# Two blocks of cached attention on one core: the last V product as loops, the identity from an iota

## The chip, the cores and the metric

The kernel runs on one core of a Trainium2 chip. The metric is the device time of one execution in microseconds (us), taken as the median of several runs; lower is better. The engines are TensorE (PE in the profile, its weight loads PEld), VectorE (DVE), ScalarE (ACT), GpSimd (POOL) and SyncE (SP), which here issues all DMAs. They run side by side and wait for each other only by semaphores.

## The reference

Two blocks, A and B, are computed one beside the other with their own inputs. Each takes one new token for 2 batch rows, projects it to 32 heads of 192, attends over a cache of 8192 tokens and projects the result back to 640:

```python
q = (x @ wq).reshape(2, 1, 32, 192)              # x: 2 x 1 x 640
scores = einsum("bhqd,bhkd->bhqk", q, k_cache) * 192 ** -0.5
p = softmax(scores)                              # over 8192 tokens
o = einsum("bhqk,bhkd->bhqd", p, v_cache)
out = o.reshape(2, 1, 32 * 192) @ wo             # 640 columns
```

All inputs are bf16; the two outputs stand side by side in 1280 columns. A K or V cache of one block holds 2 x 32 x 8192 x 192 values, about 201 MB; with four caches and the weights the kernel reads 837 MB, each byte once.

## The kernel before, in words

**Units.** The work is cut into 16 units (`NU`), one for each block, batch row and group of 8 heads (`UH`). A unit's K, and its V, is laid over the 128 partitions as 16 partitions for each head with 512 tokens in each. That row is read in three parts (`c` = 0, 1, 2) of 32768 values, 8.4 MB each: 170 whole tokens (`TC`) and 128 values of a token that is cut by the border (the fragments).

**Buffers and loads.** `big` holds three buffers of one part each. The list `loads` gives the order on SP's queue: the K parts of unit 0; then for each unit u a V part of unit u - 1 and a K part of unit u in turn; at the end the three V parts of unit 15. Each load waits until the part that lay in its buffer has been used up. Behind the last V part come the output weights `wo`: block A's in one piece, block B's in five pieces of 29, 11, 5, 2 and 1 rows. Block A's is put into the buffer of V part 0 of the last unit and waits for the signal `("pv", 15, 0)`, which the last matmul of that part gives; block B's goes into the buffer of part 1 and waits for `("pv", 15, 1)`. Last on the queue stand the two stores of the output.

**Start.** GpSimd clears the 33 columns of `tri`, clears `ident`, writes the columns of a triangle with 32 more memsets (L512 to L516), and then clears six other tiles (L518). VectorE makes the four diagonal blocks of the 128 x 128 identity `ident` by subtracting neighbouring columns of the triangle (L521). From the identity come a few small selection tiles (L526 to L548). TensorE turns x with it (L395, `pe_x`), which needs x and the identity. VectorE copies the turned x into `xz` (L292), and the projection follows (`pe_proj`, L402): 16 steps for each block, five matmuls of 384 columns in each. Step 0 is written out, steps 1 to 15 are a loop.

**Scores of a unit.** VectorE multiplies a K part in place by q (L303, L305), TensorE sums groups of 16 by matmuls with the identity (L420, L432), VectorE adds the rest (L313, L317). When all three parts are done, VectorE takes the largest score, GpSimd takes it over the partitions (L346), ScalarE takes the exponentials (L367), and VectorE spreads them into `pb`, with the columns of 8 heads for every token (L340).

**V product of a unit** (`pe_pv`, L450, L456). For each part 85 matmuls: the stationary operand is 40 columns of `pb`, which hold the weights of two tokens for 8 heads each, the moving operand is two tokens of V, 384 columns. All add into the PSUM tile `ops`. Behind the first of the 85 stand one or two small matmuls for the fragments. In the units' loop the V parts of unit u - 1 are worked between the K parts of unit u; for the last unit (`if not real`) the three parts follow each other.

**End.** After part 2 of the last unit its sums are divided by the softmax's denominator and placed into `oall` (L349 to L358, L462), turned (L471), and multiplied by `wo`: block A first (L484, 96 matmuls), then eight idle matmuls (L492), then block B piece by piece (L484, 96 matmuls). ScalarE and VectorE write each block's result to SBUF (L387, L388), and SP stores it.

**How a loop is made.** Every engine has a `_Stream`, a list of operations with their waits, signals and tags. `emit` writes the list out; for each entry `(lo, hi, period)` it is given, `_find` looks for operations whose tags run from `lo` to `hi`, and which agree in name, signals and waits. Two or more such repetitions become one hardware loop (`eng.Fori`), the rest stays unrolled. Inside a loop an operand's place is worked out from the loop's counter:

```python
    def at(self, x, n=1, mult=1):
        return slice(x, x + n) if self.base is None else bass.ds(self.base * mult + x, n)
```

TensorE has three loops before: the projection's steps 1 to 15 for each block, and units 1 to 15.

Of the kernel before, what the change touches and what calls it, by code (L numbers as in the profile page):

```python
# [5 lines left out]
ALU = mybir.AluOpType  # L6
# [113 lines left out]
def build_kernel(nc, blocks, out):  # L120
# [4 lines left out]
    UH = 8  # L125
    HG = Hn // UH
    NQB = NBLK * B
    NU = NQB * HG
    LASTU = NU - 1
    TP = Sk * UH // 128  # L130
    NCH = 3
    ROW = TP * Dh // NCH
    TC = ROW // Dh
    FR = ROW - TC * Dh
    OFF = (0, Dh - FR, FR)
# [8 lines left out]
    QW = 2 * Dh  # L144
    WR = Hn * Dh // 128
    GP = Dh // WR
    HP = 32
    MP = HP + UH
    HM = Hn // 2
    XM = HM - 1  # L150
    PQ0 = -100
    XW = XM + 128
    PO = 128 - UH
    scale = float(Dh) ** -0.5
# [3 lines left out]
    with ExitStack() as es:  # L158
# [10 lines left out]
        pb = sb("pb", [128, TP * UH], BF16)  # L169
        sc = sb("sc", [128, TP], F32)  # L170
# [3 lines left out]
        ident = sb("ident", [128, 128], BF16)  # L174
# [12 lines left out]
        rc = sb("rc", [UH, 1], F32)  # L187
# [3 lines left out]
        xz = pb[:, 0:XZE].rearrange("p (k c m) -> p k c m", k=NBLK, c=DC)  # L191
        x4 = pb[0:NQB, 1536:1536 + D]
        zero = pb[:, 2304:2304 + Dh]
        tri = pb[0:HP, 2560:2560 + HP + 1]
        out_sb = pb[0:HP + B, 0:D]
        o_all = qc[:, 0:Dh]

        ops = ps("ops", [128, 512], F32)
# [8 lines left out]
        bufs = [big[:, i * ROW:(i + 1) * ROW] for i in range(NBUF)]  # L207
# [7 lines left out]
        S_pe = _Stream("pe", sem("s_pe"), reg, 1)  # L215
        S_act = _Stream("act", sem("s_act"), reg, 1)
        S_dve = _Stream("dve", sem("s_dve"), reg, 1)
        S_pool = _Stream("pool", sem("s_pool"), reg, 1)
# [17 lines left out]
        buf = {}  # L236
# [9 lines left out]
        for blk, rows in ((0, (WR,)), (1, (29, 11, 5, 2, 1))):  # L246
            r = 0
# [32 lines left out]
        def fragments(b, c):  # L280
            if c == 0:
                return [(0, 0, FR, bufs[b][:, ROW - FR:ROW])]
            if c == 1:
                return [(0, FR, Dh, bufs[b][:, 0:Dh - FR]), (1, 0, Dh - FR, bufs[b][:, ROW - (Dh - FR):ROW])]
            return [(1, Dh - FR, Dh, bufs[b][:, 0:FR])]
# [154 lines left out]
        def col(s):  # L440
            return 64 * (s // 8) + 32 * (s % 2) + 8 * (s % 8 // 2)

        def pe_pv(u, c):
# [14 lines left out]
                return ins  # L458
            return fn

        def pe_pl(u):
            return lambda eng: eng.matmul(oacc_all[:, 0:Dh], place[:, S_pe.at(UH * u, 128, UH)], o_sb[:],  # L462
                                          start=False, stop=True, skip_group_check=True)
# [45 lines left out]
        for blk in range(NBLK):  # L509
            S_sp.add(out_dma(blk), waits=[("oev", blk, 1), ("oev", blk, 0)])  # L510

        S_pool.add(lambda eng: eng.memset(tri, 0.0), sig=("tri0",))  # L512
        S_pool.add(lambda eng: eng.memset(ident[:], 0.0))
        for n in range(1, HP + 1):
            S_pool.add((lambda n: (lambda eng: eng.memset(tri[0:n, n:n + 1], 1.0)))(n),
                       waits=[("tri0",)] if n == 1 else [], sig=("tri",) if n == HP else None)  # L516
        for n, t in enumerate((pb[:, 0:XZE], zero, esel[:], onehot[:], turn[:], place[:])):
            S_pool.add((lambda t: (lambda eng: eng.memset(t, 0.0)))(t), sig=("init", n))  # L518

        for n in range(128 // HP):  # L520
            S_dve.add((lambda r: (lambda eng: eng.tensor_tensor(ident[r, r], tri[:, 1:HP + 1], tri[:, 0:HP], ALU.subtract)))  # L521
                      (slice(HP * n, HP * n + HP)), waits=[("tri",)], sig=("id1",) if n == 128 // HP - 1 else None)
        for blk in range(NBLK):
            for b in range(B):
                S_dve.add(dve_xz(blk, b), waits=[("px",), ("init", 0)], sig=("xz",) if (blk, b) == (1, 1) else None)
        S_dve.add(lambda eng: eng.tensor_reduce(em[:], ident[:].rearrange("p (m t) -> p t m", t=GP), AXL.X, ALU.add),  # L526
                  waits=[("id1",)], sig=("em",))
# [38 lines left out]

        streams = {"pe": S_pe, "dve": S_dve, "act": S_act, "pool": S_pool}
        slots = {e: {} for e in streams}

        def put(eng, slot, name, fn, waits, lag=0):  # L570
            slots[eng].setdefault(slot, []).append((name, fn, [w for w in waits if w is not None], lag))

        for u in range(NU + 1):
            real, old = u < NU, u >= 1
            v = u - 1

            def red(c, k):
                put("dve", u, ("r", c, k), dve_red(u, c, k), [("s", u, c, k), ("sp", u - 1) if u else None])

            def turn_out():  # L580
                put("dve", u, ("rc", -1), dve_rc, [("pv", v, NCH - 1), ("of", v - 1)])
                put("dve", u, ("oh", -1), dve_ohi, [("of", v - 1)])
                put("dve", u, ("os", -1), dve_osum, [("oh", v)])
                put("act", u, ("of", -1), act_of, [("os", v), ("rc", v), ("pl", v - 1)])

            def v_part(c):
                if c == 0:
                    put("pe", u, ("l", -1), pe_l, [("exp", v), ("sp0", v), ("os", v - 1), ("rc", v - 1)])
                put("pe", u, ("pv", c, -1), pe_pv(v, c), [("v", v, c), ("sp", v) if c else None])

            if not real:
                for c in range(NCH):
                    v_part(c)
                turn_out()
                put("pe", u, ("pl", -1), pe_pl(v), [("of", v)])
                continue
            put("dve", u, ("su", 1), dve_su(u + 1), [("q", u)])
            for c in range(NCH):
                if old:
                    v_part(c)  # L600
                for k in range(NSUB):
                    if old and c == NCH - 1 and k == 3:
                        turn_out()
                    w = [("k", u, c), ("qe", u), ("sl", u - 1, NCH - 1) if u and c == 0 else None]
                    put("dve", u, ("m", c, k), dve_mul(u, c, k), w)
                    put("pe", u, ("s", c, k), pe_sum(u, c, k), [("m", u, c, k), prev(u, c, k)])
                    if old and c == NCH - 1 and k == 3:
                        put("pe", u, ("pl", -1), pe_pl(v), [("of", v)])
                    n = NSUB * c + k - 3
                    if n >= 0:  # L610
                        red(n // NSUB, n % NSUB)
                put("pe", u, ("sl", c), pe_rest(u, c),
                    [("m", u, c, NSUB - 1), ("rl", u - 1) if u and c == 0 else None])
            c = NCH - 1
            for k in range(NSUB - 3, NSUB):
                red(c, k)
            put("dve", u, ("rl",), dve_rest, [("sl", u, c)])
            put("dve", u, ("mx",), dve_max, [("rl", u)])
            put("dve", u, ("mp",), dve_mp, [("mx", u), ("ar", u - 1) if u else None, ("negm",)])
            put("dve", u, ("nm",), dve_nm, [("ar", u)])  # L620
            put("dve", u, ("nb",), dve_nb, [("nm", u), ("exp", u - 1) if u else None])
            put("pe", u, ("q", 1), pe_q, [("su", u + 1), ("qe", u)])
            put("pool", u, ("ar",), pool_ar, [("mp", u), ("nm", u - 1) if u else None])
            put("act", u, ("qe", 1), act_q, [("q", u + 1), ("m", u, NCH - 1, NSUB - 1)])
            put("act", u, ("exp",), act_exp, [("nb", u), ("l", v) if u else None])
            g0, g1 = -(-TC // 8), TP // 8
            put("dve", u, ("sp0",), dve_spread([(0, g0), (g1 - 1, g1)]),
                [("exp", u), ("pv", v, NCH - 1) if u else None, ("mask",)])
            put("dve", u, ("sp",), dve_spread([(g0, g1 - 1)]), [])

        def full(name, u):
            lag = name[-1] if name[0] in ("su", "q", "qe", "l", "pv", "rc", "oh", "os", "of", "pl") else 0
            rest_ = name[1:-1] if lag else name[1:]
            return (name[0], u + lag) + rest_

        for e, S in streams.items():
            order = [n for n, *_ in slots[e][1]]
            have = {n for n, *_ in slots[e][0]}
            after = {}
            at = None  # L640
            for n in order:
                if n in have:
                    at = n
                else:
                    after.setdefault(at, []).append(full(n, 0))
            for u in sorted(slots[e]):
                for n, fn, waits, _ in slots[e][u]:
                    S.add(fn, waits=waits, sig=full(n, u), tag=(u, n),
                          pre=after.get(None, ()) if u == 0 and n == slots[e][0][0][0] else (),
                          post=after.get(n, ()) if u == 0 else ())  # L650

# [13 lines left out]
        with nc.Block() as block:  # L665
            @block.sync
            def _(eng):
                S_sp.emit(eng)

            @block.gpsimd  # L670
            def _(eng):
                S_pool.emit(eng)

            @block.vector
            def _(eng):
                S_dve.emit(eng, [(1, NU, 1)])

            @block.scalar
            def _(eng):
                S_act.emit(eng, [(1, NU, 1)])  # L680

            @block.tensor
            def _(eng):
                S_pe.emit(eng, [(PQ0 + 1, PQ0 + HM, 1), (PQ0 + 2 * HM + 1, PQ0 + 3 * HM, 1), (1, NU, 1)])

        for blk in range(NBLK):
            nc.scalar.wait_ge(*reg["odone", blk])
# [49 lines left out]
```

## Time and profile before

| | us |
|---|---|
| median of 3 runs (lowest, highest) | 1937.39 (1936.87, 1938.21) |
| the profiled execution, whole | 1937.25 |
| its span, first to last instruction | 1935.4 |
| TensorE busy | 1532.6 |
| weight loads busy, beside the matmuls | 784.1 |
| VectorE busy | 1119.2 |
| ScalarE busy | 29.6 |
| GpSimd busy | 9.4 |

The profile is of one execution, the whole time of which is 1.85 us above its span. The time beside a group of instructions is their busy time; matmuls are pipelined, and the ends that the trace gives them are modelled, so the distance between starts says more about their pace than the length of one. "Issue" as a cause of idle time means that the engine waited for nothing that the profile shows. The granted clock is the share of full speed that TensorE's clock gate allowed, 0.929 on average over the span.

### The profile page before, as it was taken

How to read it: one execution, taken by the hardware profiler on the slowest of the kernel's cores; microseconds unless marked ns; L12 is line 12 of the kernel's file. 1: busy time of each engine (PE TensorE's matmuls, PEld its weight loads, DVE VectorE, ACT ScalarE, POOL GpSimd, SP SyncE). 2: the span in 40 equal slices, each digit the busy share in tenths (PEclk: the TensorE clock that was granted, in tenths of full speed). 3: DMA queues.
4: the chain of work that ended last, by engine and by line, in shares of the span. 5: the costliest groups of instructions: out<-in, count | busy, mean ns of one | idle time of the engine just before them, and what ended most of it. 6: DMA issues, size and time to landing. Idle time of an engine off the chain costs nothing.

```text
span 1935.4 us, 18767 instructions
## 1 busy us (share of the span) xinstructions
PE 1532.6 (79%) x8255; PEld 784.1 (41%) x8256; DVE 1119.2 (58%) x841; ACT 29.6 (2%) x75; POOL 9.4 (0%) x60
## 2 busy tenths in 40 slices
PE   4778787887888778797787878878797777878778
PEld 2334343443434434353343434433343343434435
DVE  0785555846566485546846566485546846565450
ACT  0000000000000000000000000000000000000000
POOL 0000000000000000000000000000000000000000
PEclk9999898898999999999999999999998988999889
DMA  9999999999999999999999999999999999999998
GB/s 412 435 441 434 434 436 433 433 435 433 433 435 433 433 433 433 433 433 435 437 435 435 433 433 433 433 433 433 433 434 437 435 437 433 433 433 436 433 432 380
DMA packets 15147, 836.94 MB, mean 432 GB/s; under 512 B 1688, under 2 KB 1824, under 8 KB 2208
## 3 DMA queue, kind: packets, MB, share of 16 engines
q1 hardware_dynamic: 15136, 836.78, 99.8%
q8 instruction: 9, 0.15, 0.0%
q14 instruction: 2, 0.02, 0.0%
HBM read 836.77 MB, written 0.01 MB: 432 GB/s over the span
## 4 chain that ended last, share of the span: by engine, by line
PE 35%; DMA 34%; DVE 17%; issue 13%; DVEq 0%; POOL 0%; ACT 0%; SPq 0%; ACTq 0%; POOLq 0%
PE ops L450 22%; DMA big<-in_B_k_cache_dram 17%; DMA big<-in_A_k_cache_dram 14%; DVE big L305 12%; PE scps L420 10%; DVE sc L313 3%; DMA big<-in_B_wo_dram 2%; PE scps L402 2%; PE rest L432 1%; DMA pb<-in_B_x_dram 1%; DVE pb L340 1%; DVE rmax L321 0%; POOL mg L346 0%; PE ops L456 0%; DVE o_hi L352 0%
## 5 line engine op out<-in xcount | busy, mean ns | idle before, releaser
L420 PE MATMUL scps<-big,ident 128*128 128x512 bf16 x2880 | 716.5, 408 | 284.0 <-DVE sc L313 268.1
L305 DVE TENSOR_TENSOR big<-big,qt 128x6144 bf16<-128x6144 bf16 (+1 forms) x240 | 847.5, 3548 | 0.0
L450 PE MATMUL ops<-big,pb 128*40 128x384 bf16 x4080 | 710.7, 336 | 0.0
L420 PEld LDWEIGHTS scps<-big,ident 128*128 128x128 bf16 x2880 | 285.1, 103 | 700.6 <-DVE sc L313 332.9
L450 PEld LDWEIGHTS ops<-big,pb 128*40 128x40 bf16 x4080 | 414.5, 103 | 272.3 <-issue 28.9
L303 DVE TENSOR_TENSOR pad<-big,qt 128x128 bf16<-128x128 bf16 (+1 forms) x64 | 11.9, 207 | 633.7 <-DMA big<-in_B_k_cache_dram 341.5
L313 DVE TENSOR_REDUCE sc<-scps 128x32 f32<-128x512 f32 x240 | 161.0, 681 | 31.2 <-PE scps L420 31.2
L340 DVE TENSOR_TENSOR pb<-sc,mask 128x704 bf16<-128x704 f32 (+2 forms) x96 | 76.3, 863 | 14.1 <-ACT sc L367 14.1
L438 PE MATMUL ops<-rs,mask 128*8 128x1 f32 x32 | 3.1, 167 | 84.8 <-DVE pb L340 84.8
L432 PEld LDWEIGHTS rest<-big,ident 128*128 128x128 bf16 x576 | 44.4, 101 | 13.9 <-issue 4.5
L432 PE MATMUL rest<-big,ident 128*128 128x160 bf16 x576 | 49.1, 236 | 0.0
L438 PEld LDWEIGHTS ops<-rs,mask 128*8 128x8 f32 x32 | 1.6, 90 | 88.4 <-DVE pb L340 82.8
L402 PE MATMUL scps<-big,pb 128*128 (+1 forms) x160 | 31.7, 338 | 6.8 <-issue 6.8
L358 ACT ACTIVATE o_sb<-o_hi,rc 8x192 bf16<-8x192 f32 x16 | 7.3, 454 | 1537.2 <-DVE o_hi L355 1537.2
L349 DVE RECIPROCAL rc<-ops 8x1 f32<-8x1 f32 x16 | 2.3, 147 | 41.4 <-PE ops L450 41.4
L295 DVE TENSOR_TENSOR su<-esel,onehot 128x144 bf16<-128x144 bf16 x17 | 5.1, 300 | 35.8 <-PE outps L410 35.8
L402 PEld LDWEIGHTS scps<-big,pb 128*128 (+1 forms) x160 | 15.7, 99 | 22.6 <-issue 15.1
L395 PE MATMUL rest<-ident,pb 4*128 4x4 bf16 x5 | 0.4, 178 | 21.9 <-DMA pb<-in_B_x_dram 21.9
L346 POOL PARTITION_ALL_REDUCE mg<-mp x16 | 5.8, 365 | 1855.2 <-DVE mp L324 1855.2
L317 DVE TENSOR_REDUCE sc<-rest 128x30 f32<-128x480 f32 x16 | 10.5, 657 | 7.3 <-PE rest L432 7.3
L367 ACT ACTIVATE sc<-sc,nb 128x512 f32<-128x512 f32 x16 | 11.5, 721 | 32.8 <-DVE nb L330 32.8
L292 DVE CAST pb<-rest 128x5 bf16<-128x5 f32 x4 | 0.4, 171 | 19.5 <-PE rest L395 19.5
(66 smaller groups left out, 131.5 us busy)
## 6 DMA issues: line engine op xcount, KB each, us to landing
big<-in_B_wq_dram SPq DMA_DIRECT2D x1, 7680.0 KB, 37.4
big<-in_A_wo_dram SPq DMA_DIRECT2D x1, 7680.0 KB, 29.2
big<-in_A_wq_dram SPq DMA_DIRECT2D x1, 7168.0 KB, 20.3
big<-in_B_wo_dram SPq DMA_DIRECT2D x1, 4640.0 KB, 27.7
big<-in_B_wo_dram SPq DMA_DIRECT2D x1, 1760.0 KB, 31.4
big<-in_B_wo_dram SPq DMA_DIRECT2D x1, 800.0 KB, 32.8
big<-in_A_wq_dram SPq DMA_DIRECT2D x1, 512.0 KB, 3.8
big<-in_A_k_cache_dram SPq DMA_DIRECT2D x24, 38.4
```

What stands on the lines that cost most here:

```text
L303: eng.tensor_tensor(pad[:, t, lo:hi], src, qt[:, 0, lo:hi], ALU.mult)
L305: return eng.tensor_tensor(t, t, qt[:].broadcast_to([128, size(k), Dh]), ALU.mult)
L313: return lambda eng: eng.tensor_reduce(sc[:, lo:lo + SUB], scps[bank(u, c, k)][:], AXL.X, ALU.add)
L317: eng.tensor_reduce(dst, rest[:, 0:NCH * REST, :].rearrange("p (c t) g -> p c t g", c=NCH), AXL.X, ALU.add)
L340: ins = eng.tensor_tensor(dst[:, lo:hi, a], src[:, lo:hi, a].unsqueeze(3).broadcast_to(shape), mask[:].unsqueeze(1).unsqueeze(1).broadcast ...
L346: return eng.partition_all_reduce(mg[:], mp[:], 128, bass.bass_isa.ReduceOp.max)
L358: return eng.activation(o_sb[:], o_hi[:], ACTF.Identity, scale=rc[:])
L367: return eng.activation(sc[:], sc[:], ACTF.Exp, bias=nb[:], scale=scale, accum_out=rs[:])
L402: ins = eng.matmul(flat[0][:, 0:QW], xz[:, blk, c, S_pe.at(m, 128)], wq_t[blk][:, c, S_pe.at(QW * m, QW, QW)], start=(blk == 0 and m == 0 ...
L420: ins = eng.matmul(scps[bank(u, c, k)][:], ident[:], t[:, :, j * DG:(j + 1) * DG], start=(j == 0), stop=(j == NJ - 1))
L432: ins = eng.matmul(rest[:, lo:lo + n, :], ident[:], src[:, :, j * DG:(j + 1) * DG], start=(j == 0), stop=(j == NJ - 1))
L450: ins = eng.matmul(ops[0:MP, 0:QW], pb[:, j0:j0 + MP], bufs[b][:, OFF[c] + j * QW:OFF[c] + (j + 1) * QW], start=(c == 0 and j == 0), stop= ...
```

## The change

Two edits that do not touch each other.

In the last unit, part 0 and part 1 of the V product are each split into a head (`pe_pv_head`: the first of the 85 matmuls and the fragments) and 21 passes (`pe_pv_pass`) of four matmuls. The passes carry tags of their own, from 1000 for part 0 and 1100 for part 1, and `emit` gets a range for each, so that they can become loops of 21 turns. The operands of a pass move on by 64 columns of `pb` and by 1536 columns of the V buffer at each turn. The last pass gives the signal `("pv", 15, c)`; the other passes give signals too, for which nobody waits. Part 2 stays as it was, and so do the units in the units' loop.

The identity: GpSimd writes `p - column` as f32 into the first 128 columns of `sc` with one iota, and VectorE compares it with zero into `ident` with one instruction. The tile `tri`, its 33 memsets, the memset of `ident` and the four subtractions go.

```diff
+    PV0 = 1000
+    VP = 4
+    VN = (TC // 2 - 1) // VP
...
-        tri = pb[0:HP, 2560:2560 + HP + 1]
+        diff = sc[:, 0:128]
...
+        def pe_pv_head(u, c):
+            b = buf["v", u, c]
+
+            def fn(eng):
+                j0 = col(TC * c)
+                ins = eng.matmul(ops[0:MP, 0:QW], pb[:, j0:j0 + MP], bufs[b][:, OFF[c]:OFF[c] + QW],
+                                 start=(c == 0), stop=False, skip_group_check=True)
+                for t, lo, hi, src in fragments(b, c):
+                    j0 = col(NCH * TC + t)
+                    ins = eng.matmul(ops[0:UH, lo:hi], pb[:, j0:j0 + UH], src, start=False, stop=False,
+                                     skip_group_check=True)
+                return ins
+            return fn
+
+        def pe_pv_pass(u, c, i):
+            b = buf["v", u, c]
+
+            def fn(eng):
+                for n in range(VP):
+                    j = 1 + VP * i + n
+                    ins = eng.matmul(ops[0:MP, 0:QW], pb[:, S_pe.at(col(TC * c + 2 * j), MP, 16 * VP)],
+                                     bufs[b][:, S_pe.at(OFF[c] + j * QW, QW, VP * QW)],
+                                     start=False, stop=True, skip_group_check=True)
+                return ins
+            return fn
...
-        S_pool.add(lambda eng: eng.memset(tri, 0.0), sig=("tri0",))
-        S_pool.add(lambda eng: eng.memset(ident[:], 0.0))
-        for n in range(1, HP + 1):
-            S_pool.add((lambda n: (lambda eng: eng.memset(tri[0:n, n:n + 1], 1.0)))(n),
-                       waits=[("tri0",)] if n == 1 else [], sig=("tri",) if n == HP else None)
+        S_pool.add(lambda eng: eng.iota(diff, [[-1, 128]], base=0, channel_multiplier=1,
+                                        allow_small_or_imprecise_dtypes=True), sig=("diff",))
...
-        for n in range(128 // HP):
-            S_dve.add((lambda r: (lambda eng: eng.tensor_tensor(ident[r, r], tri[:, 1:HP + 1], tri[:, 0:HP], ALU.subtract)))
-                      (slice(HP * n, HP * n + HP)), waits=[("tri",)], sig=("id1",) if n == 128 // HP - 1 else None)
+        S_dve.add(lambda eng: eng.tensor_scalar(ident[:], diff, 0.0, None, ALU.is_equal), waits=[("diff",)], sig=("id1",))
...
             if not real:
+                put("pe", u, ("l", -1), pe_l, [("exp", v), ("sp0", v), ("os", v - 1), ("rc", v - 1)])
                 for c in range(NCH):
-                    v_part(c)
+                    if c == NCH - 1:
+                        put("pe", u, ("pv", c, -1), pe_pv(v, c), [("v", v, c)])
+                        continue
+                    put("pe", u, ("pvh", c), pe_pv_head(v, c), [("v", v, c), ("sp", v) if c else None])
+                    for i in range(VN):
+                        n = ("pv", c, -1) if i == VN - 1 else ("pvt", c, i)
+                        put("pe", u, n, pe_pv_pass(v, c, i), [])
+                        tags["pe", u, n] = (PV0 + 100 * c + i, ("pvt", c))
...
-                S_pe.emit(eng, [(PQ0 + 1, PQ0 + HM, 1), (PQ0 + 2 * HM + 1, PQ0 + 3 * HM, 1), (1, NU, 1)])
+                S_pe.emit(eng, [(PQ0 + 1, PQ0 + HM, 1), (PQ0 + 2 * HM + 1, PQ0 + 3 * HM, 1), (1, NU, 1)]
+                          + [(PV0 + 100 * c, PV0 + 100 * c + VN, 1) for c in range(NCH - 1)])
```

More of the change, by code (lines that the diff above doesn't have):

```diff
@@ L151, in build_kernel @@
     PQ0 = -100
+    PV0 = 1000
+    VP = 4
+    VN = (TC // 2 - 1) // VP
+    assert VP % 4 == 0 and 1 + VN * VP == TC // 2
     XW = XM + 128
@@ L568, in build_kernel @@
         slots = {e: {} for e in streams}
+        tags = {}
         def put(eng, slot, name, fn, waits, lag=0):
@@ L647, in build_kernel @@
                 for n, fn, waits, _ in slots[e][u]:
-                    S.add(fn, waits=waits, sig=full(n, u), tag=(u, n),
+                    S.add(fn, waits=waits, sig=full(n, u), tag=tags.get((e, u, n), (u, n)),
                           pre=after.get(None, ()) if u == 0 and n == slots[e][0][0][0] else (),
```

## The prediction

> **What bounds the kernel now.** I read the page first (span, transfers, queues), then the chain of waits, then the timeline at both ends, where the change lies, and last the windows view for the clock. The page says that the transfers set the time:
>
> ```profile
> span 1935.4 us, 18767 instructions
> ...
> GB/s 412 435 441 434 434 436 433 433 435 433 433 435 433 433 433 433 433 433 435 437 435 435 433 433 433 433 433 433 433 434 437 435 437 433 433 433 436 433 432 380
> DMA packets 15147, 836.94 MB, mean 432 GB/s; under 512 B 1688, under 2 KB 1824, under 8 KB 2208
> ## 3 DMA queue, kind: packets, MB, share of 16 engines
> q1 hardware_dynamic: 15136, 836.78, 99.8%
> q8 instruction: 9, 0.15, 0.0%
> ```
>
> 836.9 MB at 432 GB/s is 1937 us, the whole span; of 40 slices only the first and the last move less. So an edit in mid-kernel is worth nothing unless it holds a transfer back, and an edit behind the last loads is worth what TensorE needs there. The V product of the last unit lies there. First its part 0 (timeline: start, length, engine, line, operation, count, in brackets the idle time before and what ended it), then what TensorE does to the end:
>
> ```profile
> 1869.19 15.40 PE L450 MATMUL ops<-big,pb 128*40 128x384 bf16 x85
> 1869.49 0.16 PEld L450 LDWEIGHTS ops<-big,pb 128*40 128x40 bf16 x1 [0.16 <-issue]
> ```
>
> ```profile
> 1884.67 13.99 PE L450 MATMUL ops<-big,pb 128*40 128x384 bf16 x85
> 1898.59 0.22 PE L456 MATMUL ops<-big,pb 128*8 128x128 bf16 x1
> 1898.74 13.83 PE L450 MATMUL ops<-big,pb 128*40 128x384 bf16 x84
> ...
> 1915.58 8.36 PE L484 MATMUL outps<-big,oT 128*2 128x320 bf16 x96
> 1924.10 1.67 PE L492 MATMUL ops<-big,ident 128*128 128x512 bf16 x7 [0.16 <-issue]
> 1926.27 5.69 PE L484 MATMUL scps<-big,oT 128*2 128x320 bf16 x80 [0.50 <-DMA big<-in_B_wo_dram]
> 1932.19 1.45 PE L484 MATMUL scps<-big,oT 128*2 128x320 bf16 x16 [0.23 <-DMA big<-in_B_wo_dram]
> ```
>
> From 1869 to 1933.6 TensorE hardly stops: parts 0, 1 and 2 of V, the last unit's sums, block A's output product, the idle matmuls, block B's output product. That the transfers still lead is seen only in the bracket before block B's product, and it holds 0.50 us. This small lead is all that hides anything added to TensorE here. Two transfers hang on parts 0 and 1, wo of block A and wo of block B. Their issues, and the times to landing:
>
> ```profile
> 1884.45 0.33 SPq L256 DMA_DIRECT2D big<-in_A_wo_dram  x1
> 1898.53 2.24 SPq L256 DMA_DIRECT2D big<-in_B_wo_dram  x5
> ```
>
> ```profile
> big<-in_A_wo_dram SPq DMA_DIRECT2D x1, 7680.0 KB, 29.2
> ...
> big<-in_A_wq_dram SPq DMA_DIRECT2D x1, 512.0 KB, 3.8
> ```
>
> Block A's wo lands at 1884.45 + 29.2 = 1913.7. Its 7680 KB (7.86 MB) take 18.2 us at 432 GB/s, so until about 1895.5 the queue still had V to move: its issue has 11 us of lead. Block B's is issued 15 us ahead of 1913.7. The 512 KB load, into an empty queue, takes 3.8 us where 432 GB/s would take 1.2; so 2.6 us is the start of a transfer.
>
> **The loops.** The change turns the 84 matmuls behind the head of part 0, and of part 1, into 21 passes of four, with addresses from the loop's counter. No matmul goes. What a pass costs beyond its matmuls is seen in the projection, such a loop on the same engine, with five matmuls of the same 384 columns in a pass (timeline, then the windows view, whose third column from the end is the granted clock):
>
> ```profile
> 22.78 6.49 PE L402 MATMUL scps<-big,pb 128*128 128x384 bf16 x30 [0.53 <-issue]
> ...
> 40.88 3.50 PE L402 MATMUL scps<-big,pb 128*128 x20 [0.26 <-issue]
> 44.64 0.98 PE L402 MATMUL scps<-big,pb 128*128 x5 [0.26 <-issue]
> ```
>
> ```profile
> 44.64:59.78 15.14, 11.84 (x60) 5.78 (x61) 0.00 (x0) 0.00 (x0) 0.00 (x0) 1.00 0.96 416
> 1868.50:1872.10 3.60, 3.60 (x14) 1.66 (x14) 2.66 (x2) 0.00 (x0) 0.00 (x0) 0.50 1.05 455
> 1849.00:1862.00 13.00, 8.72 (x43) 3.87 (x44) 11.27 (x11) 0.45 (x1) 0.00 (x0) 1.00 1.00 434
> ```
>
> Twelve passes (60 matmuls) fill 15.14 us, 1.26 us each. In part 2 above, 84 matmuls take 13.83 us with one every 0.1625 us and 0.33 us for the last, so five need 0.81 us: 0.45 us of each pass is waiting, and "issue" says that no data was missing. Inside a pass nothing waits: 0.98 is four starts of 0.1625 and the last one's 0.33. So matmuls with computed addresses are handed over every 0.16 us or faster, and the rest belongs to turning back. If handing over one takes s and the turn e, a pass of five is 5s + e = 1.26, and one of four 1.26 − s. At most s is 0.16, by what was just read. At least it is about 0.065, the pace of matmuls with fixed addresses in block B's product:
>
> ```profile
> 1926.27 3.76 PEld L484 LDWEIGHTS scps<-big,oT 128*2 128x2 bf16 x58 [0.99 <-DMA big<-in_B_wo_dram]
> ```
>
> I take s = 0.12, about the middle: **1.14 us for a pass of four**. The ends are 1.10 (s = 0.16) and 1.26 (s = 0). If all of the pass went with the number of its matmuls it would be 1.01; the gaps, which stand at the turn alone, speak against that.
>
> The Trainium skill, page "Advanced Engine Details and Errata", section "Control Flow Timing", gives about 108 ns for a compare-and-branch. By that figure alone the 40 turns below would be 4.3 us and the whole change some +3 us; the projection's 0.45 us per pass disagrees.
>
> Four matmuls need 0.65 us, so each turn leaves 0.49 us idle. 21 passes have 20 turns (entering and leaving show no gap: the 20 matmuls from 40.88 are one loop's last pass, five unrolled ones and the next loop's first two passes). Two loops: 40 × 0.49 = 19.6 us. From this goes what the slow clock hides. Part 0 starts at 0.50 of the clock with matmuls 0.32 us apart, nine of them (15.40 − 0.33 = 9 × 0.32 + 75 × 0.1625). Four at that pace last longer than a pass, so two to three turns are covered, 1.1 us. TensorE is then 18.5 us later, 8.7 from part 0 and 9.8 from part 1. Does the clock stay up when the array works 0.65 of 1.14 us, 57%? In the scores of the last unit, busy 8.72 of 13 us, it was 1.00, and in the projection, at 64%, too. I take full clock.
>
> Now who waits. Part 0's end releases wo of A on SP's queue: 1893.2 in place of 1884.45; with its start of 2.6 us it arrives just as the queue runs dry at 1895.5. Part 1's end releases the five pieces of wo of B: 1917.0 in place of 1898.5, behind A's landing at 1913.7, so the DMA engines stop there for some 6 us. On SP only the output's stores are queued behind. B's rows have landed by 1917.0 + 2.6 + 18.2 = 1937.8. TensorE asks for them later than that: part 2 ends 18.5 us late, block A's product begins at 1934.1 and the idle matmuls end at 1944.3. Block B then waits for no row: 95 × 0.065 + 0.3 = 6.5 us, where it took 7.37 (1926.27 to 1933.64). With the lead of 0.50 that gives back 1.3 us. The end moves by 18.5 − 1.3 = **17.2 us**, by TensorE's chain; the late transfer hides under it.
>
> **The identity.** It is off the path. Groups of the first 66 us, and two rows of the timeline:
>
> ```profile
> L518 POOL MEMSET pb<- 128x1430 bf16 (+1 forms) x2 | 1.5, 763 | 0.0
> L550 ACT ACT_TABLE_LOAD x1 | 1.3, 1283 | 0.7 <-PEq L722 0.7
> L515 POOL MEMSET pb<- 1x1 bf16 (+31 forms) x32 | 1.1, 91 | 0.0
> L521 DVE TENSOR_TENSOR ident<-pb 32x32 bf16<-32x32 bf16 x4 | 0.7, 166 | 2.1 <-POOL pb L515 2.1
> ```
>
> ```profile
> 3.75 0.30 POOL L518 MEMSET place<- 8x248 bf16 x1
> 21.90 0.27 PEld L395 LDWEIGHTS rest<-ident,pb 4*128 4x128 bf16 x5 [21.90 <-DMA pb<-in_B_x_dram]
> ```
>
> Its first reader waits for x until 21.90; the identity is ready at 2.1 + 0.7 = 2.8 us. 34 memsets and four subtractions go, an iota and a comparison come. The trace has no iota: by the nearest rows of GpSimd it lies between 0.09 us (a small memset) and 1.5 us (the two large ones); I take 0.5. The six memsets behind it on the same queue, done at 4.05 now, and the comparison end within 6 us. No gain and no loss reaches the end, unless the iota took some 19 us; then the cover is gone and each further us delays the projection.
>
> **Sum.** The profiled execution took 1937.25 us (the span and 1.85 around it), 0.14 below the runs' median of 1937.39. 1937.25 + 17.2 = **1954.4 us**.
>
> **Rivals.** *Turns hidden, so not slower* (0.07): the sequencer is ahead of the array and turning back costs nothing. For it: the projection's first 30 matmuls, the unrolled five and five passes, run without one gap, as the first nine of them are at half pace. Against it: every later pass has its gap. It decides at 0.65 us per pass; below, the time stays at 1937.3, and the only gain is in instructions not fetched (0.15 MB of 837 for all of them). The Trainium skill's 108 ns would end beside this case.
>
> *Half clock* (0.05): the gaps let the throttle fall. A pass then takes 4 × 0.32 = 1.28 us and a part 26.9, in place of 15.1 and 13.7; part 2 loses 1.4 in warming: 26.4 − 1.3 = +25.1, 1962.4 us. The projection's clock speaks against it.
>
> *Code fetched again* (0.03): each turn drops what was fetched ahead and waits for a transfer, at most the 3.8 us of the 512 KB load. In one of the two loops: 20 × (3.8 − 0.49) = 66 us more, about 2020. Against it: the two projection loops and the unit loop turn back 42 times, and q8 has nine packets in all. The Trainium skill, page "Runtime: NRT & Kernel Launch", section "Instruction fetch mechanics", states such a stall for targets outside the fetched window; the nine packets agree that short loops stay inside.
>
> *Slow iota* (0.01), over 19 us: above 1954. *No loop made* (0.01): if the stream's search did not find the passes alike, the code would stay unrolled, 1937.3; tag, signal and waits are the same in all 21.
>
> **How the numbers follow.** Forecast 0.83. Passes of 1.01 give 40 × 0.36 − 0.8 − 1.3 = +12.3, 1949.5 us; 1.10 gives 1952.9; 1.26 gives 40 × 0.61 − 1.4 − 1.3 = +21.7, 1959.0; half clock 1962.4. So the range is 1949 to 1962.5 and leaves out 0.12. About 0.2%, 3.9 us, is what a measurement of this kernel can tell from no change: same are the hidden turns and no loop, 0.08; slower 0.91; faster 0.01.
>
> **What would show it.** Right: groups of four matmuls 1.14 us apart in parts 0 and 1 with "issue" in the brackets; wo of A issued at 1893, wo of B at 1917, a dip in DMA from 1914; no wait for DMA before block B's product; nine packets or fewer in q8. Wrong: passes of 0.65 us; a clock near 0.5 in the loops; a first matmul that waits for the identity and not for x.

## The result and the profile after

The changed kernel takes 1952.89 us (median of 6 runs, 1951.47 to 1954.52), the kernel before 1937.16 us in the same comparison (6 runs, 1936.75 to 1938.21): ratio 1.008, 95% interval 1.0067 to 1.0093, 15.7 us slower. The prediction had 1954.4 in a range of 1949 to 1962.5. The profiled execution took 1953.05 us, its span is 1951.6.

On the page after, the transfers are the same bytes, but the last slice (48.8 us) has fallen from 380 to 243 GB/s: nothing moves from 1912 to 1916, and after 1937 next to nothing is left to move.

```profile
GB/s 423 430 430 436 431 438 431 431 441 430 438 431 433 439 430 439 430 434 438 430 439 430 435 437 433 437 430 437 435 434 434 431 437 435 434 435 430 442 426 243
DMA packets 15146, 836.93 MB, mean 429 GB/s; under 512 B 1688, under 2 KB 1824, under 8 KB 2208
## 3 DMA queue, kind: packets, MB, share of 16 engines
q1 hardware_dynamic: 15136, 836.78, 99.1%
q8 instruction: 8, 0.13, 0.0%
```

The timeline of parts 0 and 1 shows the passes (L485 is the pass's matmul, L470 the head of part 1, L454 that of part 2; the first row is eight passes in which the view shows no gap), and the windows view the clock in the same stretches (third column from the end; the last is GB/s):

```profile
1869.99 8.18 PE L485 MATMUL ops<-big,pb 128*40 x32
...
1878.44 0.82 PE L485 MATMUL ops<-big,pb 128*40 x4 [0.27 <-issue]
...
1891.71 0.82 PE L485 MATMUL ops<-big,pb 128*40 x4 [0.27 <-issue]
1892.55 0.32 PE L470 MATMUL ops<-big,pb 128*40 128x384 bf16 x1
...
1892.95 0.83 PE L485 MATMUL ops<-big,pb 128*40 x4
1894.02 0.82 PE L485 MATMUL ops<-big,pb 128*40 x4 [0.24 <-issue]
...
1915.03 0.82 PE L485 MATMUL ops<-big,pb 128*40 x4 [0.26 <-issue]
1915.76 0.33 PE L454 MATMUL ops<-big,pb 128*40 128x384 bf16 x1
```

```profile
1869.98:1875.09 5.11, 5.11 (x18) 2.51 (x18) 1.98 (x2) 0.00 (x0) 0.00 (x0) 0.50 0.95 410
1880.63:1891.70 11.07, 8.35 (x40) 3.82 (x40) 0.00 (x0) 0.00 (x0) 0.00 (x0) 1.00 0.97 420
1895.10:1915.00 19.90, 14.83 (x72) 6.89 (x72) 0.00 (x0) 0.00 (x0) 0.00 (x0) 1.00 0.81 349
1912.00:1916.00 4.00, 3.15 (x17) 1.44 (x15) 0.00 (x0) 0.00 (x0) 0.00 (x0) 1.00 0.00 0
1914.30:1918.50 4.20, 3.94 (x24) 2.15 (x24) 0.00 (x0) 0.00 (x0) 0.00 (x0) 1.00 0.49 141
```

From 1878.44 to 1891.71 lie 12 passes, 1.106 us each; from 1894.02 to 1915.03 lie 19, also 1.106. The clock is at 1.00 once the first 5 us are over, and at 0.50 in these. The last two rows are the hole in the transfers: nothing for 4 us, and 141 GB/s in the 4.2 us around the issue of block B's weights. Then the issues of the output weights, and TensorE's end:

```profile
1892.56 0.33 SPq L260 DMA_DIRECT2D big<-in_A_wo_dram  x1
1915.89 2.59 SPq L260 DMA_DIRECT2D big<-in_B_wo_dram  x5
```

```profile
1933.01 8.36 PE L514 MATMUL outps<-big,oT 128*2 128x320 bf16 x96
1941.53 1.67 PE L522 MATMUL ops<-big,ident 128*128 128x512 bf16 x7 [0.16 <-issue]
1943.13 6.68 PE L514 MATMUL scps<-big,oT 128*2 128x320 bf16 x96
```

Block B's product (L514) now runs in one piece of 96, and the bracket with the DMA wait is gone: TensorE's chain sets the end (the row of 1933.01 is block A's product). From row to row, before and after:

| step | before | after | later by | added here |
|---|---|---|---|---|
| first matmul behind part 0's head | 1869.19 | 1869.99 | 0.80 | 0.80 |
| part 0 done, wo of A issued | 1884.45 | 1892.56 | 8.11 | 7.31 |
| part 1 done, wo of B issued | 1898.53 | 1915.89 | 17.36 | 9.25 |
| idle matmuls begin (second of them) | 1924.10 | 1941.53 | 17.43 | 0.07 |
| block B's product begins | 1926.27 | 1943.13 | 16.86 | -0.57 |
| its last matmul ends | 1933.64 | 1949.81 | 16.17 | -0.69 |
| span | 1935.4 | 1951.6 | 16.2 | 0.03 |

The time outside the span was 1.45 us where it had been 1.85, so the profiled executions differ by 15.8 us.

At the start, the iota came much later than the memsets had, and x was still the last input:

```profile
9.52 0.24 POOL L542 IOTA sc<- 128x128 f32 x1 [9.09 <-issue]
9.71 1.48 POOL L545 MEMSET pb<- 128x1430 bf16 x2
9.79 1.84 DVE L547 TENSOR_SCALAR ident<-sc 128x128 bf16<-128x128 f32 x1 [9.79 <-POOL sc L542]
...
22.91 0.27 PEld L399 LDWEIGHTS rest<-ident,pb 4*128 4x128 bf16 x5 [22.91 <-DMA pb<-in_B_x_dram]
```

### The profile page after: what moved, and what is told of

It reads as the page before. It is cut to its first block, busy times and chain, and to the rows that moved or that the text cites. A ratio compares the mean times of both kernels' runs of the same rounds, so it can differ in the third digit from the quotient of the medians.

```text
span 1951.6 us, 19029 instructions
## 1 busy us (share of the span) xinstructions
PE 1547.7 (79%) x8255; PEld 787.9 (40%) x8256; DVE 1120.7 (57%) x838; ACT 29.6 (2%) x75; POOL 8.4 (0%) x27
## 4 chain that ended last, share of the span: by engine, by line
PE 41%; DMA 29%; DVE 16%; issue 13%; DVEq 0%; POOL 0%; ACT 0%; ACTq 0%; SPq 0%; POOLq 0%
PE ops L454 22%; DMA big<-in_B_k_cache_dram 14%; DMA big<-in_A_k_cache_dram 14%; PE scps L424 12%; DVE big L309 10%; DVE sc L317 3%; PE ops L485 2%; PE scps L406 2%; PE rest L436 2%; DMA pb<-in_B_x_dram 1%; DVE pb L344 1%; DVE rmax L325 1%; PE outps L514 0%; PE scps L514 0%; POOL mg L350 0%
## 5 line engine op out<-in xcount | busy, mean ns | idle before, releaser
L454 PE MATMUL ops<-big,pb 128*40 128x384 bf16 x3910 | 682.0, 336 | 0.0
L454 PEld LDWEIGHTS ops<-big,pb 128*40 128x40 bf16 x3910 | 397.3, 103 | 261.6 <-issue 28.2
L307 DVE TENSOR_TENSOR pad<-big,qt 128x128 bf16<-128x128 bf16 (+1 forms) x64 | 11.9, 206 | 616.5 <-DMA big<-in_B_k_cache_dram 333.1
L485 PE MATMUL ops<-big,pb 128*40 x168 | 36.3, 348 | 9.2 <-issue 9.2
L485 PEld LDWEIGHTS ops<-big,pb 128*40 x168 | 17.1, 102 | 28.0 <-issue 20.9
```

The source lines that it names most:

```text
L307: eng.tensor_tensor(pad[:, t, lo:hi], src, qt[:, 0, lo:hi], ALU.mult)
L454: ins = eng.matmul(ops[0:MP, 0:QW], pb[:, j0:j0 + MP], bufs[b][:, OFF[c] + j * QW:OFF[c] + (j + 1) * QW], start=(c == 0 and j == 0), stop= ...
L485: ins = eng.matmul(ops[0:MP, 0:QW], pb[:, S_pe.at(col(TC * c + 2 * j), MP, 16 * VP)], bufs[b][:, S_pe.at(OFF[c] + j * QW, QW, VP * QW)], s ...
```

## The experiments

All times are medians, beside runs of the kernel before on the same chip (1937.08 to 1937.27 us). Every diff is against the changed kernel. The theory under test: the loss is what TensorE's sequencer cannot get ahead with in the 40 turns; the rivals are the new identity, a price by matmul, a turn that always stops the array, and the late transfer.

**The two halves apart.** First the loops with the old identity:

```diff
-        S_pool.add(lambda eng: eng.iota(diff, [[-1, 128]], base=0, channel_multiplier=1,
-                                        allow_small_or_imprecise_dtypes=True), sig=("diff",))
+        S_pool.add(lambda eng: eng.memset(tri, 0.0), sig=("tri0",))
+        S_pool.add(lambda eng: eng.memset(ident[:], 0.0))
...
-        S_dve.add(lambda eng: eng.tensor_scalar(ident[:], diff, 0.0, None, ALU.is_equal), waits=[("diff",)], sig=("id1",))
...
```

> The two loops alone, the identity made as before. Theory: the whole loss sits in the turns of the two loops (40 turns with about 0.45 us idle each, less what the half clock at the start of part 0 and the lead before block B's product hide), so +15 to +16 us against before, the same as the full change. Rival: the new start (x landed at 22.9 and not at 21.9 us in the changed kernel, and the last unit's V product began 0.8 us later) is part of it, then about +14.5 us and x back at 21.9.

Measured: 1952.82 us, ratio 1.0079 (1.0065 to 1.0093), the whole loss. Then the identity alone:

```diff
                 for c in range(NCH):
-                    if c == NCH - 1:
-                        put("pe", u, ("pv", c, -1), pe_pv(v, c), [("v", v, c)])
-                        continue
...
+                    v_part(c)
```

> The identity alone, the V product unrolled as before. Theory: nothing to see, within 0.5 us of before, although the iota begins only at about 9.5 us; the first matmul still waits for x. Rival: +0.8 to +1.0 us, with x landing a microsecond later, if the late start of GpSimd's first iota takes something from the transfers.

Measured: 1937.33 us, ratio 0.9999 (0.9990 to 1.0008), although its iota began at 9.80 us and x was used at 22.90, as in the full change. The identity adds nothing; the rival that gave it a microsecond is out.

**Longer passes.** Same matmuls, fewer turns.

```diff
-    VP = 4
+    VP = 12
```

> Passes of 12 matmuls, 7 passes, 6 turns in each loop. From passes of five (1.262 us, projection) and four (1.105 us, the changed kernel) the theory has 0.157 us for each matmul and 0.48 us for a turn: a pass of 12 takes 2.36 us, 0.41 idle at each turn, 2.5 us for part 1, about 0.7 for part 0, less 1.25 of lead: +2 us against before. Rival: the cost goes with the number of matmuls that have computed addresses, whatever the number of turns; then a pass takes 3.3 us and the end moves by +14 us as with passes of four.

Measured: 1939.44 us, ratio 1.0012 (1.0003 to 1.0021), +2.2 us. The timeline: part 0 in one row, in part 1 a first row of three passes without a gap, then single ones from 1893.39 to 1900.43, three periods of 2.347 us.

```profile
1870.15 16.57 PE L485 MATMUL ops<-big,pb 128*40 x84
...
1886.96 6.19 PE L485 MATMUL ops<-big,pb 128*40 x36
1893.39 2.12 PE L485 MATMUL ops<-big,pb 128*40 x12 [0.24 <-issue]
...
1900.43 2.12 PE L485 MATMUL ops<-big,pb 128*40 x12 [0.24 <-issue]
```

The slope between passes of 4 and 12 is (2.347 - 1.106) / 8 = 0.155 us for a matmul, and 0.48 is left for the turn: the theory's numbers, and no price by matmul alone. That the first passes of part 1 show no gap says that the sequencer was still ahead from part 0, where in this trace 17 matmuls were 0.32 us apart.

```diff
-    VP = 4
+    VP = 28
```

> Passes of 28 matmuls, 3 passes, 2 turns in each loop. Theory: a pass of 28 x 0.157 + 0.48 = 4.87 us against 4.55 without loop, 0.3 idle at a turn, part 0 wholly covered by the half clock, part 1 +0.65 us, which is less than the 1.25 us of lead: no change against before, within 0.5 us. Rival (cost by matmul): +14 us again.

Measured: 1936.81 us, ratio 1.0000 (0.9991 to 1.0009). Part 1 is one row, as long as unrolled (13.83 us for part 2 before): no turn shows.

```profile
1884.69 13.83 PE L485 MATMUL ops<-big,pb 128*40 x84
```

**What a turn consists of.** Passes of four whose operands do not move; all but four of the 84 column pairs are left out.

```diff
-                    ins = eng.matmul(ops[0:MP, 0:QW], pb[:, S_pe.at(col(TC * c + 2 * j), MP, 16 * VP)],
-                                     bufs[b][:, S_pe.at(OFF[c] + j * QW, QW, VP * QW)],
+                    ins = eng.matmul(ops[0:MP, 0:QW], pb[:, col(TC * c + 2 * j):col(TC * c + 2 * j) + MP],
+                                     bufs[b][:, OFF[c] + j * QW:OFF[c] + (j + 1) * QW],
```

> Both loops with passes of four as in the change, but every pass uses the operands of the first one (it leaves out all but four of the 84 column pairs), so that no address is worked out in the loop. It tells what a turn consists of. Theory: the 0.48 us sit in the turn itself (count, compare, jump, fetch), the 0.157 us of each matmul in its address; then a pass takes about 4 x 0.065 + 0.48 = 0.74 us, 0.09 us idle, and the end moves by +1 us or less. Rival: the idle time stands at the turn because TensorE must run dry there whatever the pass holds; then passes stay at 1.1 us and the end moves by +15 us.

Measured: 1936.49 us, ratio 0.9998 (0.9988 to 1.0008), and part 1 at the unrolled pace:

```profile
1885.40 13.83 PE L485 MATMUL ops<-big,pb 128*40 128x384 bf16 x84
```

So 21 turns alone cost nothing, and the rival (the array runs dry at every turn) is out. Since the array's 0.65 us hide the pass here, two shorter passes were measured, with the same fixed operands.

```diff
-    VP = 4
+    VP = 1
...
```

> Both loops with one matmul in a pass, 84 passes each, all with the operands of the first (it leaves out the other 83 column pairs). Passes of four with fixed operands had run at the unrolled pace, so the price of a bare turn was hidden there. Theory: a turn without any address work still takes about 0.4 us; a pass then takes about 0.45 us, a part 38 us in place of 13.7, and the end moves by about +45 us. Rival: a bare turn costs 0.1 us or less and all of the loss was address work; then a pass takes the matmul's 0.1625 us and nothing moves.

Measured: 1971.26 us (one run), +34 us, not +45. Part 1:

```profile
1903.43 32.23 PE L485 MATMUL ops<-big,pb 128*40 128x384 bf16 x84
```

(32.23 - 0.33) / 83 = 0.384 us for a pass of one. With two:

```diff
-    VP = 4
+    VP = 2
...
```

> The same with two matmuls in a pass, 42 passes. Theory: 0.50 us for a pass against 0.325 without loop, 41 turns with 0.18 idle in each loop, some 3 us of them hidden: +11 to +12 us. The difference to passes of one is the price of handing over a matmul with fixed operands, 0.03 to 0.065 us. Rival (turn of 0.1 us or less): nothing moves.

Measured: 1940.82 us (one run), +3.7 us, a third of what was expected. Not all of it is the loops': they cost 2.8 us (part 0 takes 15.6 us in place of 15.1, part 1 16.0 in place of 13.7), and in this trace the last unit's passes began at 1871.56, 2.4 us later than before.

```profile
1887.57 16.12 PE L485 MATMUL ops<-big,pb 128*40 128x384 bf16 x84
```

(16.12 - 0.1625 - 0.33) / 41 = 0.381 us for a pass of two. The bare turn is thus 0.38 us, and handing over a matmul with fixed operands costs so little that a second one does not show; the 0.03 to 0.065 us that I had expected for it were too much. Last, half of the address work (the weights' columns stay those of the first pass):

```diff
-                    ins = eng.matmul(ops[0:MP, 0:QW], pb[:, S_pe.at(col(TC * c + 2 * j), MP, 16 * VP)],
+                    ins = eng.matmul(ops[0:MP, 0:QW], pb[:, col(TC * c + 2 * j):col(TC * c + 2 * j) + MP],
```

> Both loops with passes of four, the V operand from the counter, the weights' operand fixed (it leaves out the other weight columns), so half of the address work. Theory: a matmul is handed over in about 0.11 us, a pass takes 0.48 + 4 x 0.11 = 0.92 us, 0.27 idle at a turn: 5.4 us in part 1, 3.6 in part 0, less 1.25 of lead: +8 us, 1945. Rival: any computed address makes TensorE run dry at the turn, then +15.7 us as with both; or the work is done once a pass and not for each matmul, then +1 us or less.

Measured: 1945.91 us, ratio 1.0044 (1.0027 to 1.0061), +8.8 us, where the theory had +8.

```profile
1890.63 18.78 PE L485 MATMUL ops<-big,pb 128*40 x84
```

(18.78 - 3 x 0.1625 - 0.33) / 20 = 0.898 us for a pass. Both rivals are out: the price grows with the number of computed operands. Whether it matters which of the two is computed was not tried.

The kept traces also record the instructions of TensorE's own queue, which the views leave out, and they show the turn directly. In part 1 of the change the weight loads of a pass start 0.153 us apart (median), each behind an address instruction of 0.074 us; with one computed operand the figures are 0.124 and 0.046. Between passes stand a count of 0.036 us and a compare-and-branch of 0.207 to 0.208 us, and only where operands are computed an address instruction more. From the last weight load of a pass to the first of the next it is 0.629 us with two computed operands, 0.509 with one and 0.383 in the passes of one with none.

**Where it reaches the end.** The idle matmuls ahead of block B's product taken away:

```diff
-            if n == 0:
-                S_pe.add(pe_idle, waits=[("of", LASTU)])
```

> The change without the eight idle matmuls ahead of block B's product. Theory: TensorE's chain sets the end, so their 1.8 us are on it: 1951.1 us, 1.8 less than the change. Rival: the transfers set the end (wo of block B was issued 17 us later), then nothing is gained; or the clock falls in the pause and takes the gain back.

Measured: 1950.39 us (4 runs, 1949.48 to 1952.36), 2.5 us less than the change; 1.8 had been expected, and the two sets of runs spread by some 3 us. The two profiled runs (1949.48 and 1953.05) differ by 3.6: the idle matmuls make 1.8 of it, and 1.7 are block A's product, 6.68 us here and 8.36 in the change. The granted clock tells them apart (the first row is the change, the second this run); why the clock fell in one and not in the other is not shown.

```profile
1933.00:1937.00 4.00, 3.99 (x36) 2.12 (x38) 0.00 (x0) 0.25 (x2) 0.00 (x0) 0.57 0.78 317
1933.00:1937.00 4.00, 3.96 (x60) 2.60 (x62) 0.00 (x0) 0.28 (x2) 0.00 (x0) 1.00 0.77 314
```

What filled a wait before is now on the path, which speaks for TensorE's chain and against the late transfer. It stays well above the kernel before, ratio 1.0071 (1.0054 to 1.0088).

Part 0 alone as a loop:

```diff
-                    if c == NCH - 1:
-                        put("pe", u, ("pv", c, -1), pe_pv(v, c), [("v", v, c)])
+                    if c >= 1:
+                        put("pe", u, ("pv", c, -1), pe_pv(v, c), [("v", v, c), ("sp", v)])
...
-                          + [(PV0 + 100 * c, PV0 + 100 * c + VN, 1) for c in range(NCH - 1)])
+                          + [(PV0 + 100 * c, PV0 + 100 * c + VN, 1) for c in range(1)])
```

> Only part 0 as a loop of passes of four, parts 1 and 2 unrolled, the new identity. Theory: part 0 costs 7.3 us in the trace of the change (its end 23.2 us behind its start, and 15.9 before), the lead of 1.25 us is given back once: +6.0 us against before. Rival: if the two loops shared what they hide unevenly, or if the late wo of block A stopped the transfers, another sum: +4 or +8 us.

Measured: 1944.61 us, ratio 1.0035 (1.0023 to 1.0048): +7.5 us, with an interval of +4.5 to +9.3 that holds the theory's sum and one rival's. The time does not tell them apart, but the trace does:

```profile
1871.55 4.93 PE L485 MATMUL ops<-big,pb 128*40 x20
...
1894.40 0.32 PE L454 MATMUL ops<-big,pb 128*40 128x384 bf16 x1
1894.81 13.99 PE L454 MATMUL ops<-big,pb 128*40 128x384 bf16 x85
...
1935.60 6.68 PE L514 MATMUL scps<-big,oT 128*2 128x320 bf16 x96
```

Part 0 takes 22.85 us from its first pass to the head of part 1, where it took 15.07 before (1869.19 to 1884.26), so its loop costs 7.8 us (theory 7.3); part 1 has its 13.99 us again, and block B's product waits for no row. Less 1.26 of lead that makes 6.5. The profiled run is 8.3 us above that of before; the rest is mostly that its last unit's passes began 2.4 us later.

**The start.** The six memsets ahead of the iota:

```diff
-        S_pool.add(lambda eng: eng.iota(diff, [[-1, 128]], base=0, channel_multiplier=1,
-                                        allow_small_or_imprecise_dtypes=True), sig=("diff",))
         for n, t in enumerate((pb[:, 0:XZE], zero, esel[:], onehot[:], turn[:], place[:])):
             S_pool.add((lambda t: (lambda eng: eng.memset(t, 0.0)))(t), sig=("init", n))
+        S_pool.add(lambda eng: eng.iota(diff, [[-1, 128]], base=0, channel_multiplier=1,
+                                        allow_small_or_imprecise_dtypes=True), sig=("diff",))
```

> The change with the six memsets ahead of the iota on GpSimd. The iota began at 9.5 us with 9.1 us of idle before it, and the comparison took 1.84 us while the large memset ran on GpSimd. Theory: the wait of about 8.8 us starts when GpSimd comes to the iota, so it begins near 11.6 us; and the comparison, with GpSimd at rest, takes 0.2 to 0.3 us. Rivals: the wait runs from the program's start whatever stands ahead, iota at 9.5 us; the comparison's 1.84 us are its own price. The end stays at that of the change, 1953 us, in all cases.

Measured (one run, 1955.46 us, 2.6 above the change where none was expected; its last unit's passes began at 1871.83, 1.8 us later than in the change, a shift that other traces have too):

```profile
13.47 0.24 POOL L544 IOTA sc<- 128x128 f32 x1 [10.68 <-issue]
13.74 0.23 DVE L547 TENSOR_SCALAR ident<-sc 128x128 bf16<-128x128 f32 x1 [13.74 <-POOL sc L544]
```

GpSimd's pause begins when it comes to the iota, not at the program's start, and lasted 10.7 us. The comparison takes 0.23 us with GpSimd at rest and took 1.84 with a memset running there.

At last the cover itself: the six memsets ahead of the iota again, and sixteen more.

```diff
+        for n in range(16):
+            S_pool.add(lambda eng: eng.memset(pb[:, 2560:4096], 0.0), waits=[("late", n - 1)] if n else [], sig=("late", n))
```

> The change with the six memsets and sixteen more of 128 x 1536 (about 1.4 us each, 22 us) ahead of the iota, so that the identity is ready at about 34 us, 11 to 12 us behind x. Theory: the projection starts that much later, but the transfers still have work queued, so the end moves by 0 to +4 us against the change. Rival: each microsecond behind x goes through to the end, +11 us.

Measured: 1962.18 us (4 runs, 1961.73 to 1965.98), 9.3 us above the change. The identity was ready at 36.4 us, and its first reader no longer waited for x; it started 13.6 us later than in the change (36.51 against 22.91). My expectation of 0 to +4 was wrong, and the rival nearer. The windows view of the first units shows how it gets to the end (last column GB/s). It is of the slowest of the four runs, 1965.98 us, 12.9 above the profiled run of the change; of the two rows of 200 us the first is this run, the second the change:

```profile
90.00:100.00 10.00, 7.17 (x27) 3.00 (x28) 10.00 (x9) 0.00 (x0) 0.00 (x0) 0.83 0.74 317
...
120.00:130.00 10.00, 8.90 (x48) 4.17 (x46) 10.00 (x6) 0.00 (x0) 0.00 (x0) 0.97 0.78 315
...
160.00:170.00 10.00, 10.00 (x53) 4.99 (x52) 7.44 (x4) 0.00 (x0) 0.00 (x0) 1.00 0.81 316
0.00:200.00 200.00, 133.32 (x672) 64.95 (x673) 103.90 (x99) 3.65 (x8) 24.88 (x28) 0.95 0.97 409
0.00:200.00 200.00, 142.44 (x704) 69.00 (x705) 113.73 (x102) 3.66 (x8) 2.93 (x12) 0.94 1.00 430
```

Three stretches of 10 us carry 315 to 317 GB/s, where the change has 419 to 433. Over the first 200 us it is 409 and not 430, so some 10 us of transfers are lost there. That the buffers are freed later and the loads wait for them fits these rows and is argued. The last unit's passes began 12.4 us later than in the change (1882.37 against 1869.99), nearly all of the 13.6.

## Why the prediction was right, and by how much its terms were off

**The chain.** All its steps are in the trace: passes with "issue" in the brackets, wo of A at 1892.6 (predicted 1893.2), wo of B at 1915.9 (1917.0), a hole in the transfers from 1912 to 1916 (predicted from 1913.7, some 6 us), no DMA wait before block B's product, 8 packets in q8. The two loops made TensorE 7.31 + 9.25 = 16.6 us later (predicted 18.5), and the lead and the saved waits gave back 0.57 + 0.69 = 1.26 (1.3; the prediction's own terms, 0.50 and 7.37 - 6.5, make 1.4, and the product took 6.68 and not 6.5). The last unit's V began 0.8 us later, which cannot be tied to either edit: with the loops alone its passes began at 1871.24, with the identity alone at 1871.45, so this start shifts by some 2 us from run to run. The prediction has no term for it, and by luck it made up for part of what the loops fell short of: 16.6 - 1.3 alone would be +15.3, not 17.2.

**The size of a pass.** The mis-sized term is s, what the sequencer needs for one more matmul of a pass: I took 0.12 between 0.065 and 0.16, it is 0.155 to 0.157. So a pass takes 1.106 us and not 1.14 (1.118 in the traces with the memsets first, with the late identity and with part 0 alone), near the lower of the two ends given, and part 1 costs 20 x (1.106 - 0.65) = 9.1 of its 9.25 us, where I had 9.8. The lower bound of 0.065 came from unrolled matmuls with fixed operands; what paced them was not tested, and in a loop with fixed operands the sequencer needs about 0.02 us for one more.

**What the slow clock hides.** I took 1.1 us for part 0 and it hid more: 9.1 - 7.3 = 1.8 us (1.6 by TensorE's own rows, 22.56 us from the first pass to the head of part 1 in place of 15.07). The nine matmuls at half pace cost the unrolled part 9 x 0.16 = 1.4 us. The loop does not pay them, because the sequencer sets its time: part 0 takes 22.56 us, nearly the 22.81 of part 1, where the clock is full. How long the slow stretch lasts does not matter either. With the loops alone it was 2.9 us and not 5.1, and five passes ran without a gap and not eight, but the part took 22.59 us:

```profile
1871.24 4.93 PE L485 MATMUL ops<-big,pb 128*40 x20
...
1893.83 0.32 PE L470 MATMUL ops<-big,pb 128*40 128x384 bf16 x1
```

**What a turn is.** Here the reading was incomplete. "The rest belongs to turning back" held for the place of the idle time, not for its cause. A bare turn takes 0.38 us and is hidden by four matmuls of 0.65 in all, as the fixed operands show. What exposes it is that a matmul with two computed operands is handed over in 0.155 us, nearly as long as the array takes for it (0.1625): the sequencer then gains next to nothing on the array inside a pass, and the turn, 0.48 us with the address work that belongs to it, stands idle almost whole (0.456). One computed operand gives 0.898 us, in between. The Trainium skill, page "Advanced Engine Details and Errata", section "Control Flow Timing", names about 108 ns for a compare-and-branch; a whole bare turn with its count and its matmul is 0.38 us here, so that figure covers less than a third of it; the compare-and-branch that the trace records takes 0.207 us by itself, about twice the figure, and the measured one counts here.

**The rivals.** Hidden turns came true only with passes of 28 or with fixed operands in passes of four. Half clock did not: 1.00 in both loops at 0.65 busy of 1.11. Code was not fetched at every turn: 8 packets for 40 more turns. Of the identity's two bounds the upper was wrong: the iota itself took 0.24 us, but the pause ahead of it some 9 us, where I had at most 1.5 for both; the six memsets behind it ended at 11.9 us and not by 6. The cover of 19 us held it, with 11.3 us to spare (11.63 to 22.91). That cover is real: with the late identity, which began the projection 13.6 us later, 9.3 us reached the end by the medians and 12.9 in the profiled runs.

**Spread.** The changed kernel's runs spread by 3.1 us, those of before by 1.5. Before, waits for transfers sat between the last unit and the end; with the chain on TensorE nothing is left to take up a late start. This is argued from the rows and was not measured by itself, and the five runs with the loops alone, which spread by only 0.7 us, do not bear it out.

## What to carry to other kernels

Here a loop on TensorE was free where the sequencer kept ahead of the array. With fixed operands it needs less than the array for a pass of four; with passes of 28 it needs some 4.8 us (28 x 0.155 + 0.48, an estimate) where the array needs 4.55, and with two such turns in each part its lead lasted. With another loop, see whether idle "issue" stands once a pass, measure two lengths of pass, and split the time into a part for each matmul and one for each turn. Fewer and longer passes (28 here) or operands that do not move brought the cost to nothing in this kernel. In a kernel bound by transfers, look for the last bracket that still names a DMA: its length is all that hides work added on the engine behind it.

## What the runs showed of the hardware that was not expected

- The one iota of these programs costs GpSimd a pause of 8.7 to 10.7 us, counted from when GpSimd comes to it; what a second one would cost was not tried. The kept traces record two MODIFY_POOL_CONFIG instructions right ahead of it, which the views leave out, and the pause lies behind them: from 0.83 to 9.52 us in the change, from 2.86 to 13.47 with the memsets first, from 25.69 to 35.90 with the late identity. The Trainium skill, page "GPSIMD Engine Reference", section "2.1 Instruction dispatch", puts the first call of a freshly loaded GpSimd kernel at approximately 6 us with no visible instruction; the kind agrees, the measured pause is longer and counts here.
- A comparison of 128 x 128 f32 on VectorE took 0.23 us with GpSimd at rest and 1.84 us beside two GpSimd memsets of 1.48 us together.
- A pass of one and a pass of two matmuls with fixed operands both take 0.38 us (one run each).
- The clock's slow start varies: the matmuls at 0.32 us lasted 2.9 us in the trace of before and 5.1 us in that of the change, and again 2.9 with the loops alone. In the loops this costs nothing, because a pass at half clock (4 x 0.32) is hardly longer than one that waits for the sequencer.
